# Reordering an S4 convolution's forward and backward pass on one Trainium2 core: K's chain and y first, lag sums and slabs beside dW2, every stage in a written order

## The chip, the cores and the metric

The kernel runs on one core of a Trainium2 chip. A core has engines with an instruction stream each: PE (matrix products; a weight load, PEld, comes before each matmul), DVE (elementwise and reductions), ACT (elementwise with a function), POOL (general) and SP, which in this kernel issues the DMA transfers. Each engine works its stream in order, and semaphores make one wait for another. SBUF is the memory on the core with 128 partitions, PSUM the small memory that PE writes to, DRAM the memory outside.

The metric is the device time of one execution in microseconds (us). The kernel before takes 954.58 us (median of 3 runs, 954.05 to 956.04).

## The reference

The forward pass normalizes its input, runs an S4 convolution and a two-layer network on it and multiplies the two; the kernel computes the output and the gradients of all eleven inputs.

```python
def _A_ref(u, A_re, A_im, B_re, B_im, C_re, C_im, log_dt, Dskip):
    dt = jnp.exp(log_dt)[:, None]
    logdA = dt * (A_re + 1j * A_im); dB = dt * (B_re + 1j * B_im)
    P = jnp.exp(logdA[:, :, None] * l[None, None, :])
    K = jnp.einsum("dn,dnl,dn->dl", Cc, P, dB).real
    ...
    Yf = Uf * Kf[None, :, :, :]
    y = irfft2(Yf)[..., :L]
    return y + u * Dskip

x = A_u                                # 2048 x 512
xn = _layernorm(x, axis=-1)
s = _A_ref(xn, ...)
g = _silu(_silu(xn @ w1) @ w2)         # w1: 512 x 1792, w2: 1792 x 512
return x + s * g
...
out, vjp = jax.vjp(_f, A_u, A_A_re, ..., B_w1, B_w2)
return (out, *vjp(grad_out))
```

## The kernel before, in words

Positions (2048) lie as 16 tiles t of 128 rows, channels d are 512, states n are 128. The long convolution is done with matmuls against cosine and sine tables: `TFd` for the way forward (four parts kt of 1 MB), `TId` for the way back. Both are built in the first stage and kept in DRAM.

*Stage 1* (`stage_1`, 0 to 204 us): layer norm, the network forward (L540, L515; the pre-activation h goes to DRAM as `hTd`, the transposed activation as `akd`), the tables, and powers of the state matrix, `XYd` in DRAM: 28 rows of 512 channels, real and imaginary. DS = grad_out * g is kept in SBUF.

*Stage 2* (`stage_2`): transforms of xn (`fwd_classes`, L647) and of DS (`fwd_eo`, L672) for each kt, evicted by ACT (L648, L674); DVE makes XU and XD (`rad4` L79 to L86, `add_eo` L681 to L686), stores them as `UXd` and `DXd`, and multiplies them (`cplx_mul` L94 to L98) into BK.

*Stage 3* (`stage_3`): the inverse transform of BK is the gradient of K, dK (`inv_mm` L697, eviction L828). `gs` sums it over groups of lags with selector matmuls (L818); the sums go through DRAM (`dKgd`) into `Gt`. Beside it, chunks of the table of powers are built.

A *chunk* is a quarter of the channels (32 channels by 4 positions in the layout). `ld_xy` loads its 28 rows, `chunk_tables` spreads them with nine ACT copies (L883 to L895) over X (41 columns), Y and C (16 each), and fills the rest with complex products on DVE (L902 to L904, L920). `chunk_K` multiplies C and X on PE (256 matmuls of 41 columns a chunk, L939, evicted at L941, put in order at L945) into the convolution kernel K, which goes through DRAM (`store_K` L955, `load_K` L964 to L987) into `K_b`. The layout is X[p, c, q, h, e] with c real or imaginary, q the channel group, h the column and e a parity, so what PE reads of one q lies densely.

*Stage 4* (`stage_4`, 361 to 624 us): 16 *slabs*, four a chunk, in class `Slabs`. Slab i transposes 16 groups of X and 8 of Y on PE (`P1`, L1012 and L1020; evictions L1014, L1021), builds a block matrix from Gt (`Gb`, L1029), multiplies the two (`P2`, L1041, eviction L1043), multiplies by Y on DVE (`D3`, L1052 and L1055), and sums (`P3`, L1070); results go to DRAM (`Snd`). Between the slabs stand the remaining chunks, K's way through DRAM, DMA transposes of w1 and w2 (`wt_phases`, L1098, L1102, L1107), and, from slab 10 on, K's transform (`KTransform`): the same tiles and products as for xn, with result BY.

*Stage 7* (`stage_7`): y from BY with the skip added (L694, L697), then DO = s-side gradient and the first output.

*Phase 3* (`phase_3`): here the order isn't written out; a scheduler of the framework sets it. `gen_dw2` (dW2, L1410, with akd loaded again) is mixed with `gen_conv_g` (product of KXd and DXd, inverse transform, into DXC); then `gen_ffn_bwd` (L1478 dh, transposes L1436, L1446 dx, layer norm backward), with dh kept whole in SBUF; then `gen_dw1` (L1502, eviction L1504, store `out_dram<-o10b`) and the small parameter gradients `gen_ssm_final`.

In the other stages each engine's order is the order in which the Python text emits instructions. All DMAs are issued by SP in that order, so a transfer whose data isn't ready holds those behind it. Tiles with the same `tag` share buffers: a new one waits until the last user of the old one is done. PSUM has two double tiles (`pd`) and three single ones (`ps`).

Of the kernel before, what the change touches and what calls it, by code (L numbers as in the profile page):

```python
# [124 lines left out]
def kernel(ctx, tc, A_u, A_A_re, A_A_im, A_B_re, A_B_im, A_C_re, A_C_im, A_log_dt, A_Dskip, B_x, B_w1, B_w2, grad_out,  # L125
# [20 lines left out]
    k.XYd = dr.tile([P, NT, 2, D], BF16, name="XYd")  # L146
    k.akd = dr.tile([FT, P, T, P], BF16, name="akd")
    k.hTd = dr.tile([4, P, FT, 512], BF16, name="hTd")
    k.W1Td = dr.tile([P, FT, D], BF16, name="W1Td")
    k.W2Td = dr.tile([P, DK, F], BF16, name="W2Td")  # L150
# [4 lines left out]
    k.Snd = dr.tile([2, 2, D, N], F32, name="Snd")  # L155
    k.xn = k.const.tile([P, T, D], BF16, name="xn")
    k.left = Stack(k, "left"); k.right = Stack(k, "right")
    with tc.manual_schedule():
        stage_1(k)
        stage_2(k)  # L160
        stage_3(k)
        stage_4(k)
        stage_7(k)
    phase_3(k)
    k.right.close("do")

# [78 lines left out]

class Setup:


    def __init__(self, k, W1, W2, pr, p1):
# [33 lines left out]
        k.masks = gen_masks(k, pr)  # L283
        next(k.masks)
# [38 lines left out]
    def lam(self):  # L323
        nc, k = self.k.nc, self.k
        perm = lambda ap: ap.rearrange("p (e s j w b) -> p s e j b w", e=2, s=2, j=NJ, w=4)
        pv = lambda t: t[:].rearrange("p (j s b w e) -> p s e j b w", e=2, s=2, j=NJ, w=4)
        k.lam = self.pr.tile([P, D], F32, name="lam")
        t1 = self.p1.tile([P, D], F32, name="par_t")
        nc.vector.tensor_tensor(out=t1[:], in0=k.dtb[:], in1=k.par["A_re"], op=ALU.mult)
        for s_ in range(2):  # L330
            for e_ in range(2):
                nc.scalar.activation(out=pv(k.lam)[:, s_, e_], in_=perm(t1[:])[:, s_, e_], func=ACT.Exp)
# [56 lines left out]
def power_phases(k, pr, bs, par):  # L389


    nc = k.nc
    TT = nc.vector.tensor_tensor
    perm = lambda ap: ap.rearrange("p (e s j w b) -> p s e j b w", e=2, s=2, j=NJ, w=4)
    pv = lambda t: t[:].rearrange("p (j s b w e) -> p s e j b w", e=2, s=2, j=NJ, w=4)
    SE = [(s, e) for s in range(2) for e in range(2)]
    lam = k.lam; tau = pr.tile([P, D], F32, name="tau")
    Ctr = pr.tile([P, D], F32, name="Ctr"); Cti = pr.tile([P, D], F32, name="Cti")
# [6 lines left out]
    def setup0():  # L405
        t1 = W2_("prt", "f", 2)
        nc.vector.scalar_tensor_tensor(out=t1[:, 1], in0=k.dtb[:], scalar=1.0 / (2 * math.pi), in1=g("A_im"), op0=ALU.mult, op1=ALU.mult)
        for s, e in SE:
            nc.vector.tensor_copy(out=pv(tau)[:, s, e], in_=perm(t1[:, 1])[:, s, e])

    def setup1():
# [3 lines left out]
        for (o, ba, bb, op) in ((Ctr, 0, 1, ALU.subtract), (Cti, 1, 0, ALU.add)):  # L415
            t = W2_("prt", "s", 2)
            TT(out=t[:, 0], in0=g("C_re"), in1=dB[:, ba], op=ALU.mult)
            TT(out=t[:, 1], in0=g("C_im"), in1=dB[:, bb], op=ALU.mult)
            for s, e in SE:
                TT(out=pv(o)[:, s, e], in0=perm(t[:, 0])[:, s, e], in1=perm(t[:, 1])[:, s, e], op=op)  # L420
        one = bs.tile([P, 2, 2, D], BF16, name="one", tag="XYg", bufs=2)
        nc.gpsimd.memset(one[:, 0, 0], 1.0); nc.gpsimd.memset(one[:, 0, 1], 0.0)
        nc.gpsimd.tensor_copy(out=one[:, 1, 0], in_=Ctr[:]); nc.gpsimd.tensor_copy(out=one[:, 1, 1], in_=Cti[:])
# [27 lines left out]

    def S(i):
        for j, o in st.pop(i):
            nc.sync.dma_start(k.XYd[:, j], o)

    def C(i):
        w, s = st.pop(i)
        o = bs.tile([P, 2, 2, D], BF16, name="XYg", tag="XYg", bufs=2)
        nc_ = sum(e in CEXP for e in PAIRS[i])
        if nc_ == 0:  # L460
            for c, src in ((0, w), (1, s)):
                TT(out=o[:, :, c], in0=ex[i][:], in1=src[:], op=ALU.mult)
        else:
            for c, src in ((0, w), (1, s)):
                TT(out=src[:], in0=ex[i][:], in1=src[:], op=ALU.mult)
                nc.scalar.copy(out=o[:, :, c], in_=src[:])
        st[i] = [(XIDX[e], o[:, j]) for j, e in enumerate(PAIRS[i])]
        if nc_:
            oc = bs.tile([P, 2, 2, D], BF16, name="XYg", tag="XYg", bufs=2)
            bc = lambda t: t[:].unsqueeze(1).to_broadcast([P, nc_, D])  # L470
            for c in range(2):
                c1 = W2_("c_1", "f", 2); c2 = W2_("c_2", "r", 1)
                TT(out=c1[:, 0:nc_], in0=w[:, 0:nc_], in1=bc((Ctr, Cti)[c]), op=ALU.mult)
                TT(out=c2[:, 0:nc_], in0=s[:, 0:nc_], in1=bc((Cti, Ctr)[c]), op=ALU.mult)
                TT(out=oc[:, 0:nc_, c], in0=c1[:, 0:nc_], in1=c2[:, 0:nc_], op=(ALU.subtract, ALU.add)[c])
# [84 lines left out]

def stage_1(k):
    lo, ro = k.left, k.right
    k.DS = lo.open("ds").tile([P, T, D], BF16, name="DS")
    fp = ro.open("fp"); fs = ro.open("fs", 2)
    pr = lo.open("pr"); p1 = lo.open("p1")
    W1 = fp.tile([P, DK, F], BF16, name="W1", tag="W1")
# [29 lines left out]
    put(30, lambda: next(k.masks))  # L596
# [4 lines left out]
    last = max(at)  # L601
    for n, _ in enumerate(gf, 6):
        for fn, a in at.pop(n, ()):
            fn(*a)
        if n == 28:
            TF0 = fp.tile([P, DK, F], BF16, name="TF0", tag="W1")
            k.TF0 = TF0[:].rearrange("p k f -> p (k f)")[:, 0:T * 2 * P].rearrange("p (t c q) -> p t c q", t=T, c=2)
            k.nc.sync.dma_start(k.TF0, k.TFd[0])
        if n == last:
            lo.close("bs", "tab", "pr")  # L610
            stage_2_open(k)
    assert not at


def ld_tf(k, pool, kt):
    TFs = pool.tile([P, T, 2, P], BF16, name="TFs", tag="TFs")
    k.nc.sync.dma_start(TFs[:], k.TFd[kt])
    return TFs


def ld_ti(k, pool, t0):
    ti = pool.tile([P, TS, 8, P], BF16, name="TIs", tag="TIs")
    k.nc.sync.dma_start(ti[:], k.TId[:, t0:t0 + TS])
    return ti
# [14 lines left out]
def fwd_classes(k, pool, src, TFs):  # L639

    nc = k.nc
    A = pool.tile([P, 2, 4, W], BF16, name="dA", tag="dA")
    for t1 in range(4):
        ps = k.pd.tile([P, 2, W], F32, name="ps_f", tag="pd")
        for c in range(2):
            for j in range(4):
                nc.tensor.matmul(out=ps[:, c, :], lhsT=TFs[:, t1 + 4 * j, c, :], rhs=src[:, t1 + 4 * j, :], start=(j == 0), stop=(j == 3))  # L647
        nc.scalar.copy(out=A[:, :, t1, :], in_=ps[:])  # L648
    return A


def fwd_eo(k, pool, src, TFs, TN, odd=True):

    nc = k.nc
    A = pool.tile([P, 2, 2, 2, W], BF16, name="dEO", tag="dA")
# [10 lines left out]
    for (eo, i), rows in plan.items():  # L666
        ps = k.pd.tile([P, 2, W], F32, name="ps_f", tag="pd")
        for c, terms in enumerate(rows):
            n = 0
            for t1, tab in terms:  # L670
                for j in range(4):
                    nc.tensor.matmul(out=ps[:, c, :], lhsT=tab(j), rhs=src[:, t1 + 4 * j, :], start=(n == 0), stop=(n == 4 * len(terms) - 1))  # L672
                    n += 1
        nc.scalar.copy(out=A[:, eo, :, i, :], in_=ps[:])  # L674
    return A
# [13 lines left out]
def inv_mm(k, ps, B, TIs, t0, kts, add=None, last=True):  # L689

    nc = k.nc
    for j in range(TS):
        if add is not None:
            nc.tensor.matmul(out=ps[:, j, :], lhsT=k.scI[:], rhs=add[:, j, :], start=True, stop=False)  # L694
        for kt in kts:
            for c in range(2):
                nc.tensor.matmul(out=ps[:, j, :], lhsT=TIs[:, j, 2 * kt + c, :], rhs=B[:, kt, c, (t0 + j) % 4, :],  # L697
                                 start=(add is None and kt == 0 and c == 0), stop=(last and kt == kts[-1] and c == 1))


def stage_2_open(k):
    k.fw = k.left.open("fw")
    k.fw2 = k.left.open("fw2", 2)


def stage_2(k):

    nc = k.nc
    fw, fw2, ro = k.fw, k.fw2, k.right
    w = lambda nm, shp: fw.tile(shp, BF16, name=nm, tag=nm)  # L710
    psd = k.ps.tile([P, DK, P], F32, name="ps_dsk", tag="pz", bufs=1)
    st = {}

    def front(kt):
        TFs = k.TF0 if kt == 0 else TF.pop(kt)
        st["U"] = fwd_classes(k, fw2, k.xn, TFs)
        TN = neg_tf(k, fw, TFs, kt >= 2)
        if kt < 3:
            TF[kt + 1] = ld_tf(k, fw2, kt + 1)
        return TFs, TN  # L720

    TF = {}
    fr = front(0)
    for kt in range(4):
        TFs, TN = fr
        XU, XD = w("XU", [P, 2, 4, W]), w("XD", [P, 2, 4, W])
        E, O = w("r4_e", [P, 2, 2, W]), w("r4_o", [P, 2, 2, W])
        rad4(nc, XU[:, :, 0:2], XU[:, :, 2:4], st["U"], E, O, False)
        A = fwd_eo(k, fw2, k.DS, TFs, TN, kt >= 2)
        if kt == 0:  # L730
            ro.close("fs", "fp")
            k.sa = ro.open("sa"); k.xyr = ro.open("xyr"); bk = ro.open("bk"); k.tip = ro.open("tip", 3)
            B = k.BK = bk.tile([P, 4, 2, 4, W], BF16, name="BK")
            wl, ws = wt_phases(k, fw)
        for t in range(T):
            nc.tensor.matmul(out=psd[:, kt], lhsT=k.DS[:, t, kt * P:(kt + 1) * P], rhs=k.xn[:, t, kt * P:(kt + 1) * P], start=(t == 0), stop=(t == T - 1))
        if kt < 3:
            fr = front(kt + 1)
        if kt == 0:
            k.XYc = {0: ld_xy(k, k.xyr, 0)}  # L740
        nc.sync.dma_start(k.UXd[kt], XU[:])
        add_eo(nc, XD, A, None if kt >= 2 else w("r4_o", [P, 2, 2, W]))
        if kt == 2:
            k.TI = {t0: ld_ti(k, k.tip, t0) for t0 in (0, 2, 4)}
        for i in range(2 * kt, min(2 * kt + 2, 7)):
            wl(i)
            if i:
                ws(i - 1)
        PX = cplx_mul(nc, fw, XU, XD, conj_a=True)
        nc.sync.dma_start(k.DXd[kt], XD[:])  # L750
# [809 lines left out]
```

## Time and profile before

| | us |
|---|---|
| median of 3 runs | 954.58 |
| the profiled execution | 952.84 |
| its span, first to last instruction | 951.1 |
| PE, DVE, ACT, POOL busy | 687.8, 658.3, 485.8, 42.0 |
| DMA | 153.91 MB, mean 162 GB/s |

"Busy" is the union of the times in which an engine executes something. A line such as `L1014 ACT COPY XT<-pt_xt 82x1024 ... x54 | 50.8, 1021 | 0.7 <-PE pt_xt` names the source line, engine, operation, tiles and shape, the count, the busy us in total and the mean ns of one, then the idle time just before such instructions and what ended it. "issue" is a wait for nothing that the profile shows. The clock of PE that was granted in the span is 0.88 of full speed on average.

### The profile page before, as it was taken

Reading aid. Unit: us, or ns where it says so; the run is one execution under the profiler, and the core shown is the slowest. Engines: PE = TensorE matmul, PEld = TensorE weight load, DVE = VectorE, ACT = ScalarE, POOL = GpSimd, SP = SyncE. Lnnn points to the kernel's source line nnn. Section 1 sums busy time; section 2 is a strip of 40 time slices with the busy share of each in tenths; the row PEclk is TensorE's granted clock in tenths of the full one; section 3 lists DMA queues with packets and bytes.
Section 4 is the critical chain, followed back from the end, with each engine's and each line's share of the span. In section 5 each row is a group of like instructions: output and inputs, shape, how many; then the busy total and the mean of one; then the engine's idle time right before and its main releaser. Section 6 shows DMA issues by size and latency. Waiting matters only on the chain.

```text
span 951.1 us, 13819 instructions
## 1 busy us (share of the span) xinstructions
PE 687.8 (72%) x5440; PEld 359.5 (38%) x5498; DVE 658.3 (69%) x1020; ACT 485.8 (51%) x606; POOL 42.0 (4%) x48
## 2 busy tenths in 40 slices
PE   5777676899986583425476656267668999999994
PEld 2434343444432243424363332023223445555442
DVE  7897567667979997639893187955398136777760
ACT  4578696855462446749494342213101257776341
POOL 1262211000000000000000000000000000000000
PEclk9889797999997885857698788679989999999997
DMA  8547654897584916070164423579987543332520
GB/s 246 204 149 263 234 188 159 299 333 185 175 260 138 192 27 40 12 124 12 31 173 92 132 94 110 204 290 319 361 305 235 170 125 103 95 106 57 142 62 30
DMA packets 135263, 153.91 MB, mean 162 GB/s; under 512 B 64026, under 2 KB 101021, under 8 KB 130845
## 3 DMA queue, kind: packets, MB, share of 16 engines
q1 hardware_dynamic: 135197, 153.01, 53.6%
q8 instruction: 43, 0.70, 0.3%
q14 instruction: 23, 0.19, 0.1%
HBM read 85.33 MB, written 63.98 MB: 157 GB/s over the span
## 4 chain that ended last, share of the span: by engine, by line
PE 33%; DVE 29%; ACT 16%; DMA 12%; issue 5%; SPq 2%; another core or an unknown queue 1%; POOL 0%; DVEq 0%; ACTq 0%; POOLq 0%
PE ps_f L672 8%; PE ps_v L697 5%; PE ps_da L1478 4%; PE ps_dx L1446 3%; PE ps_f L647 3%; ACT XT L1014 2%; DVE m L902 2%; DVE m L903 2%; DMA TFs<-TFd 2%; DMA out_dram<-o10b 2%; DMA TIs<-TId 1%; PE ps_h L540 1%; DVE cm_t L94 1%; DMA hTd<-hs 1%
## 5 line engine op out<-in xcount | busy, mean ns | idle before, releaser
L674 ACT CAST dEO<-ps_f 128x1024 bf16<-128x1024 f32 x32 | 32.1, 1013 | 74.1 <-PE ps_f L672 44.8
L672 PE MATMUL ps_f<-K_b,TFs 128*128 128x512 bf16 x156 | 42.6, 426 | 36.3 <-DMA TFs<-TFd 18.5
L1410 PE MATMUL ps_w<-DO_all,A_ft 128*128 128x512 bf16 x219 | 53.6, 401 | 17.4 <-DMA A_ft<-akd 16.8
L697 PEld LDWEIGHTS <-TIs 128*128 128x128 bf16 x384 | 39.2, 102 | 59.8 <-issue 20.2
L540 PE MATMUL ps_h<-XNT,W 128*128 128x512 bf16 x216 | 60.0, 421 | 2.1 <-ACT hs L543 1.2
L672 PEld LDWEIGHTS <-TFs 128*128 128x128 bf16 x296 | 30.6, 104 | 80.8 <-issue 32.6
L1012 PE MATMUL pt_xt<-ident_bfloat,X 128*82 128x128 bf16 x512 | 38.4, 232 | 30.6 <-ACT XT L1014 28.5
L1502 PE MATMUL ps_w<-dh_all,xn 128*128 128x448 bf16 x256 | 51.3, 364 | 9.8 <-ACT o10b L1504 9.8
L515 PE MATMUL ps_o<-W,aT 128*128 128x512 bf16 x215 | 52.5, 384 | 1.5 <-ACT o L519 0.9
L1478 PE MATMUL ps_da<-DOT,W2T 128*128 128x512 bf16 x216 | 52.3, 379 | 0.8 <-DVE DOT L71 0.3
L1446 PE MATMUL ps_dx<-W1T,dhT 128*128 128x512 bf16 x218 | 52.4, 379 | 0.4
L1052 DVE TENSOR_TENSOR T<-Vb,YT 128x2048 bf16<-128x2048 bf16 x16 | 19.5, 1221 | 47.7 <-PE ps_S L1070 33.0
L1014 ACT COPY XT<-pt_xt 82x1024 bf16<-82x1024 bf16 x54 | 50.8, 1021 | 0.7 <-PE pt_xt L1012 0.6
L1012 PEld LDWEIGHTS <-X 128*82 128x82 bf16 x512 | 34.0, 127 | 39.5 <-issue 39.4
L1479 DVE TENSOR_TENSOR dhT<-ps_da,sd 128x1024 bf16<-128x1024 f32 x28 | 34.2, 1221 | 18.6 <-PE ps_da L1478 15.0
L1410 PEld LDWEIGHTS <-A_ft 128*128 128x128 bf16 x224 | 22.6, 103 | 47.7 <-DMA A_ft<-akd 19.2
L121 ACT ACTIVATE sd<-hsb 128x1024 bf16<-128x1024 bf16 x28 | 29.4, 1057 | 19.1 <-DVE dhT L1479 18.1
L1502 PEld LDWEIGHTS <-xn 128*128 128x128 bf16 x256 | 25.7, 100 | 35.3 <-issue 13.2
L697 PE MATMUL ps_v<-BK,TIs 128*128 128x512 bf16 x125 | 31.9, 408 | 9.7 <-DVE BK L85 8.1
L941 ACT CAST Kt<-ps_k 128x328 bf16<-128x328 f32 x16 | 12.9, 939 | 49.8 <-PE ps_k L939 36.7
L1412 ACT CAST o11b<-ps_w 128x512 bf16<-128x512 f32 x14 | 8.2, 585 | 56.3 <-PE ps_w L1410 53.8
L672 PE MATMUL ps_f<-DS,TFs 128*128 128x512 bf16 x134 | 32.3, 393 | 3.2 <-ACT dEO L674 3.2
(316 smaller groups left out, 1585.0 us busy)
## 6 DMA issues: line engine op xcount, KB each, us to landing
TIs<-TId SPq DMA_DIRECT2D x24, 512.0 KB
hTd<-hs SPq DMA_DIRECT2D x28, 256.0 KB
akd<-ak SPq DMA_DIRECT2D x28, 256.0 KB
TFs<-TFd SPq DMA_DIRECT2D x7, 1024.0 KB
XYc<-XYd SPq DMA_DIRECT2D x4, 1792.0 KB
A_ft<-akd SPq DMA_DIRECT2D x14, 512.0 KB
hsb<-hTd SPq DMA_DIRECT2D x28, 256.0 KB
XYd<-XYg SPq DMA_DIRECT2D x25, 256.0 KB
```

Of the source, the lines that this page charges most:

```text
L515: nc.tensor.matmul(out=pso[:], lhsT=aT[:, ft, tt * P:(tt + 1) * P], rhs=W2[:, ft, :], start=(ft == 0), stop=(ft == FT - 1))
L540: nc.tensor.matmul(out=ps[:, j], lhsT=W1[:, dk, ft * P:(ft + 1) * P], rhs=XNT[:, dk], start=(dk == 0), stop=(dk == DK - 1))
L672: nc.tensor.matmul(out=ps[:, c, :], lhsT=tab(j), rhs=src[:, t1 + 4 * j, :], start=(n == 0), stop=(n == 4 * len(terms) - 1))
L674: nc.scalar.copy(out=A[:, eo, :, i, :], in_=ps[:])
L697: nc.tensor.matmul(out=ps[:, j, :], lhsT=TIs[:, j, 2 * kt + c, :], rhs=B[:, kt, c, (t0 + j) % 4, :], start=(add is None and kt == 0 and c ...
L1012: nc.tensor.transpose(out=pt[0:NR, j, :], in_=X[:, c, q0 + 8 * h + j].rearrange("p h e -> p (h e)"), identity=k.ident[:])
L1014: (nc.vector.tensor_copy if n < dv else nc.scalar.copy)(out=XT[0:NR, c, 8 * h:8 * h + 8], in_=pt[0:NR])
L1410: nc.tensor.matmul(out=ps[:], lhsT=A_ft[:, t, :], rhs=k.DO[:, t, :], start=(t == 0), stop=(t == T - 1))
L1446: nc.tensor.matmul(out=psx[:], lhsT=dhT[:, ft, tt * P:(tt + 1) * P], rhs=W1T[:, ft, :], start=(ft == 0), stop=(ft == FT - 1))
L1478: nc.tensor.matmul(out=ps[:, j], lhsT=W2T[:, dk, ft * P:(ft + 1) * P], rhs=DOT[:, dk], start=(dk == 0), stop=(dk == DK - 1))
L1479: TT(out=dhT[:, f0:f0 + 2, :], in0=ps[:], in1=sd[:], op=ALU.mult)
L1502: nc.tensor.matmul(out=ps[:], lhsT=k.xn[:, t, dk * P:(dk + 1) * P], rhs=dh_all[:, t, f0:f0 + FC], start=(t == 0), stop=(t == T - 1))
```

## The change

The diff replaces most of the text from the tables on. Its parts:

1. The sequence of stages is new, and all of it is written out. Tables, K and all transposes of X and Y come first (`stage_2`), then K's transform (`stage_3`), y mixed with the transforms of DS (`stage_4`), the inverse for dK with lag sums, then dW2 mixed with the convolution's gradient and the slabs (`stage_5`), then the network's backward pass and dW1 (`stage_6`).
2. XYd and the chunk tables have another layout, X[p, h, e, c, q]: DMAs write it directly, ACT's copies go, and what PE reads of one q has 128 elements (256 bytes) between neighbours.
3. XT and YT are made early and stored in DRAM (`XTd`, `YTd`); the slabs load them. YT takes 32 transposes of 32 columns a slab in place of 8 of 128.
4. dh goes to DRAM (`dhd`) and comes back in four column blocks for dW1. The copies of w1 and w2 in DRAM go; DMA transposes write W1T and W2T where they are used. The last quarter of dx is mixed into dW1.
5. ACT issues part of the DMAs (half of K's, all of dW2's loads).
6. Smaller: permutations of the parameters in eight pieces in place of four; masks and selectors built later; layer norm backward takes its row sum on DVE with the addition and no longer on ACT.

```diff
     with tc.manual_schedule():
         stage_1(k)
-        stage_2(k)
-        stage_3(k)
+        stage_3(k, *stage_2(k))
         stage_4(k)
-        stage_7(k)
-    phase_3(k)
+        stage_5(k)
+        stage_6(k)
...
+def ld_tab(k, b):
+    slot, cys = k.slot[b % 2]
+    X = t["X"] = slot.tile([P, NH, 2, 2, 64], BF16, name="X", tag="X")
...
+    for o, i, n in ((X[:, 0:9], 0, 9), (X[:, 16:21:4], 9, 2), (X[:, 24:31:2], 11, 4), (X[:, 32:41:8], 15, 2), (Y[:, 1:4], 17, 3), (Y[:, 0:16:4], 20, 4),
+                    (CY[:, 0:16:4], 24, 4)):
+        dma(o, k.XYd[:, i:i + n, b])
...
 def chunk_tables(k, t):
+    for o, a, b, n in ((slice(9, 16), 8, slice(1, 8), 7), (slice(17, 20), 16, slice(2, 7, 2), 3), (slice(21, 24), 20, slice(2, 7, 2), 3),
+                       (slice(25, 32, 2), 4, slice(24, 31, 2), 4), (slice(33, 34), 32, slice(8, 9), 1),
+                       (slice(34, 36), 32, slice(16, 21, 4), 2), (slice(36, 40), 32, slice(24, 31, 2), 4)):
+        TT(out=m1, in0=all_(X, al).to_broadcast([P, n, 256]), in1=all_(X, b), op=ALU.mult)
+        for c in range(2):
+            TT(out=ecq(m2)[:, :, :, c], in0=part(X, al, 1 - c).to_broadcast([P, n, 2, 64]), in1=part(X, b, c), op=ALU.mult)
+        TT(out=part(X, o, 0), in0=ecq(m1)[:, :, :, 0], in1=ecq(m1)[:, :, :, 1], op=ALU.subtract)
+        TT(out=part(X, o, 1), in0=ecq(m2)[:, :, :, 0], in1=ecq(m2)[:, :, :, 1], op=ALU.add)
...
 def chunk_K(k, b, t, pool, tag):
-                            nc.tensor.matmul(out=psk[z:z + 32, gi, :], lhsT=lt.rearrange("p l e -> p (l e)"), rhs=X[:, c, q_, :, e],
+                            nc.tensor.matmul(out=psk[z:z + 32, gi, :], lhsT=CY[:, :, :, c, q_].rearrange("p l e -> p (l e)"), rhs=X[:, :, e, c, q_],
...
+            yield
...
+def gen_xt(k, xs, i, dv):
...
+                nc.tensor.transpose(out=pt[0:NR, j, :], in_=X[:, :, :, c, q0 + 8 * h + j].rearrange("p h e -> p (h e)"), identity=k.ident[:])
+            n += 1
+            (nc.vector.tensor_copy if n > 4 - dv else nc.scalar.copy)(out=XT[0:NR, c, 8 * h:8 * h + 8], in_=pt[0:NR])
+            if n == 4:
+                nc.sync.dma_start(k.XTd[i], XT[0:NR])
+            yield
...
+def stage_2(k):
+    ld_tab(k, 1)
...
+    for b in range(2):
+        for _ in front(b):
+            if k.nt0 < 6:
+                next(k.gt[0]); k.nt0 += 1
+    for b in range(NB):
+        Kg = chunk_K(k, b, k.tabs[b], k.ps, "ps")
+        Tn = k.gt[b + 1] if b < 3 else None
+        sl = [x for i in range(4 * b, 4 * b + 4) for x in (gen_xt(k, k.xs, i, 0),) * 4] + [gen_yt(k, k.xs, i) for i in range(4 * b, 4 * b + 4)]
+        if b == 3:
+            for _ in Kg:
+                pass
+            break
+        for j, g in enumerate(sl):
+            if j == 2:
+                next(k.gt[b], None)
+            next(g)
+            if j % 2 == 0:
+                next(Kg, None)
+            if b == 0 and j in (1, 3):
+                radix(j // 2)
+            if j % 3 == 2 and j > 2:
+                next(Tn)
+        next(Tn)
+        if b < 2:
+            ld_tab(k, b + 2)
+    fr = front(2)
+    store_K(k)
...
+    load_K(k, K_b)
+    next(k.gt[3])
...
+    for _ in fr:
+        pass
+    radix(2)
+    for _ in front(3):
+        pass
+    radix(3)
...
+def stage_3(k, K_b, sl):
...
+    for n, _ in enumerate(gen_kt(k, kq, K_b, UX)):
+        for g in (next(sl, None) for _ in range(3)):
+            if g is not None:
+                next(g)
...
+def stage_4(k):
+    gd = gen_d(k, k.bk, k.kq)
...
+    for t0 in range(0, T, TS):
+        if t0 % 4 == 0:
+            for _ in range(2):
+                next(gd)
...
+        inv_mm(k, ps, [k.BY[:, i] for i in range(4)], TI, t0, (0, 1, 2, 3), add=y.ins[t0]["XD"])
+        if t0 and t0 + 2 < T:
+            y.pre(t0 + 2)
...
+        o = y.out(t0, S_s)
+        if t0 + 4 < T:
+            y.load(t0 + 4)
+        nc.sync.dma_start(*o)
+        if t0 % 4 == 0:
+            next(gd); next(gd)
+        elif t0 + 2 < T:
+            for _ in range(3):
+                next(gd)
...
+def stage_5(k):
...
+        inv_mm(k, ps, k.BK, k.TI.pop(t0), t0, (0, 1, 2, 3))
...
+        if t0 % 4 == 0:
+            pr.mul(kt)
+        else:
+            pr.rad(kt, BG[:, kt])
...
+        if t0 >= 2:
+            gs(t0 - 2)
...
+    for ft in range(FT):
+        t0 = 2 * (ft - 3)
+        if 0 <= t0 < T:
+            if t0 + 2 < T:
+                skip(t0 + 2)
+            conv(t0)
+            some(1)
+        for _ in w2.run(ft):
+            some(2 if t0 >= 0 else 0)
+        some(2 if t0 >= 0 else 0)
+        if ft % 2 == 1:
+            j = ft // 2
+            nc.sync.dma_start_transpose(k.W2T[:, :, 256 * j:256 * j + 256], k.ins["w2"][256 * j:256 * j + 256])
...
+    def steps(self):
+        self.Gb(0)
+        for i in range(16):
+            self.P2(i, 0)
+            if i + 1 < 16:
+                self.Gb(i + 1)
+            yield
+            self.P2(i, 1)
+            if i + 2 < 16:
+                self.load(i + 2)
+            yield
+            self.D3(i)
+            if i:
+                self.P3(i - 1)
+            if i > 1 and i % 4 == 1:
+                self.store(i // 4 - 1)
+            yield
...
+def stage_6(k):
...
+    for n in range(28):
+        B.dh(n)
+        if n < 7:
+            nc.sync.dma_start_transpose(W1T[:, 2 * n:2 * n + 2], k.ins["w1"][:, 256 * n:256 * n + 256])
+        next(prev, None)
+        if n == 25:
+            ld_ch(0)
+        if n % 7 == 6:
+            if n < 27:
+                B.dot(n // 7 + 1)
+            for _ in prev:
+                pass
...
+            prev = B.dx(n // 7, B.dhT)
...
+    for i in range(4):
+        for dk in range(DK):
+            next(prev, None)
+            for t in range(T):
+                nc.tensor.matmul(out=ps[:], lhsT=k.xn[:, t, dk * P:(dk + 1) * P], rhs=ch[i][:, t, :], start=(t == 0), stop=(t == T - 1))
+            nc.scalar.copy(out=ob[:], in_=ps[:])
+            next(prev, None)
...
+        if i + 2 < 4:
+            ld_ch(i + 2)
```

In the excerpt, `gen_kt` and `gen_d` yield after each forward tile, after the additions, after the product and after the radix step of a part kt; `w2.run` yields in the middle of its 16 matmuls; `some(n)` runs n steps of the slabs; `front` yields after each of its four tiles; `B.dh` makes two blocks of dh and sends the ones before to DRAM.

## The prediction

> **What bounds the kernel now.** I first read the busy times of the whole span: no engine is above 72%, so no single engine is the limit and the waits between stages have to be found.
>
> ```profile
> span 951.1 us, 13819 instructions
> PE 687.8 (72%) x5440; PEld 359.5 (38%) x5498; DVE 658.3 (69%) x1020; ACT 485.8 (51%) x606; POOL 42.0 (4%) x48
> ```
>
> Then I cut the span at its stages. The columns are length, busy time and instruction count of each engine, clock, DMA share and GB/s. The cuts are: feed-forward pass, transforms of xn and DS, gradient of K with lag sums, tables and slabs (361 to 500), K's transform with slabs (500 to 624), y, dW2 with the convolution's gradient, backward, dW1.
>
> ```profile
> core 0: us, PE busy (x) PEld busy (x) DVE busy (x) ACT busy (x) POOL busy (x), PEclk, DMA share, GB/s
> 0.00:204.00 204.00, 146.41 (x901) 78.30 (x919) 153.80 (x288) 144.89 (x186) 41.13 (x44) 0.90 0.67 225
> 204.00:303.00 99.00, 86.33 (x424) 40.27 (x432) 82.40 (x106) 46.39 (x49) 0.91 (x4) 0.93 0.69 201
> 303.00:361.00 58.00, 38.73 (x424) 18.41 (x428) 54.95 (x95) 28.87 (x34) 0.00 (x0) 0.85 0.55 116
> 361.00:500.00 139.00, 67.31 (x1729) 54.37 (x1729) 103.83 (x162) 96.24 (x113) 0.00 (x0) 0.73 0.41 68
> 500.00:624.00 124.00, 64.35 (x485) 31.34 (x488) 80.45 (x95) 40.47 (x42) 0.00 (x0) 0.79 0.41 139
> 624.00:673.00 49.00, 36.49 (x141) 14.76 (x142) 25.73 (x39) 13.75 (x14) 0.00 (x0) 0.90 0.84 296
> 673.00:770.00 97.00, 82.63 (x355) 36.14 (x364) 51.40 (x56) 15.25 (x21) 0.00 (x0) 0.95 0.73 256
> 770.00:888.00 118.00, 115.42 (x736) 60.98 (x749) 79.68 (x135) 80.98 (x106) 0.00 (x0) 1.00 0.31 88
> 888.00:951.00 63.00, 50.09 (x251) 24.95 (x249) 26.06 (x48) 18.96 (x46) 0.00 (x0) 0.92 0.30 79
> ```
>
> The hole is 361 to 624: 263 us in which the busiest engine, DVE, works 184. The backward stage (115 of 118 on PE) holds nothing to win. The waits in 361 to 470 (total us, times, longest) and the longest pieces of the chain say why:
>
> ```profile
> PEld L939 <- issue: 39.6, 11, 12.8
> ACT Kt L941 <- PE ps_k L939: 27.2, 4, 14.2
> PE ps_k L939 <- DVE CY L904: 19.5, 2, 12.6
> ```
> ```profile
> 372.16 12.99 another core or an unknown queue
> ...
> 489.02 10.72 DMA TFs<-TFd
> ...
> 610.49 5.78 DMA TIs<-TId
> 616.29 8.21 DMA TIs<-TId
> ```
>
> K's small matmuls (L939) stand in PE's queue until the table products on DVE are done, or starve with nothing to wait for; K's way through DRAM and the load of its table, then the first loads of y, end the other gaps.
>
> **The change, stage by stage.** I sum the busiest engine in each new stage with the durations of this trace, add the waits that the new order leaves, and so walk through the span.
>
> *Feed-forward pass, now 204 us.* The parameter permutations get twice the instructions on half the elements (8 more on DVE near L420's 0.38 us, 4 more on ACT near 0.42): at most 5 us, beside 50 us of idle DVE; the mask building (about 5 us of small DVE operations at 1.6 us) leaves the start. I take 0, bounds -2 to +5. Three table steps of chunk 0 (7 us of DVE) now lie in its last ticks.
>
> *Tables, K, and the transposes, new: 204 to 358.* Table work on DVE per chunk: rows fit 0.154 us + elements/1.92 GHz (1024: 0.68, 2048: 1.22). Products for X: 18432 elements in 35 instructions, 15.0; C and Y, 5.4 each: 25.8 us, against 26.8 before. On ACT the nine copies that spread a chunk (L883 to L895, about 9.5 us) are gone, since seven DMAs write the layout; but all 16 XT evictions (L1014, 1.02) come to ACT, with 4 of YT (1.03), 4 of K (0.94) and 1.85 of K's reordering: 26 us. Four DMAs of 672 KB and four of 256 KB per chunk store XT and YT for later, and 1.8 MB are loaded, about 10 us at the 200 to 230 GB/s of before's load of the same bytes (405 to 416 us). PE first runs xn's transforms (64 matmuls at 0.216, 14 us), waits for chunk 0 until 227 (load landed about 207, then 20 us of products), then: chunk 0 with the products of chunk 1 and two radix steps (5.3 each) 37 us of DVE; two rounds of 26 + 6, as the load of chunk 2 and 3 starts only when a slot is free and DVE has 6 us of nothing: chunk_K(3) at 327, done 336. K's round trip took 32 us before (467.6 to 500); its 22 loads now go out on SP and ACT together and the table is loaded already: I take 22, to 358, bounds 15 to 32. ACT issues half of them, so the evictions of the last 14 us of xn's transforms queue behind; they are not late for anything until K_b is there.
>
> *K's transform, 358 to 451.* Four forward tiles (48 matmuls, 10.4 us) with 12 transposing steps on ACT: 22. Then per part on DVE: additions 4.0 (L681 to L686), product 7.2 (2.29 + 4 x 1.22, L94 to L98), radix 5.3: 16.5 x 4 = 66, plus 2.5 where PE and ACT still have 8 steps, 2.7 for y's first two preparations. 93.
>
> *y with DS, 451 to 550.* DVE per pair of y tiles: 16.5 for one part of DS (15 for the last two) and 2 x 3.4 for y (five operations at 0.68): four pairs 90. PE needs 79 (368 matmuls). 5 at the start, where y(0) has only PE, 4 for loads: about 25 MB in 99 us, 250 GB/s, where y moved 296 before and waited. The sum is 99, bounds 92 to 110. The old y (49) and DS's half of 204 to 303 go away.
>
> *Gradient of K, dW2, convolution, slabs, 550 to 720.* Inverse and lag sums need 180 matmuls (39 us), beside DVE's products for the convolution (50, and 5 for the selectors) and 12 MB of loads: PE 45. Three dW2 tiles (10) cover the way of the sums through DRAM; this was masked before, and I leave 6 uncovered. Then per dW2 tile: convolution 18 x 0.216 = 3.9, dW2 3.45, 1.67 slabs at 2.34 (ps_V 18.7 and ps_S 18.7 over 16) = 3.9; 8 tiles 90, three more 20. Sum 170. DVE needs 69 there (Gbd 1.36, T 2.6 per slab), ACT 52, so both hide. What hides them is PE; without it, 58 us of slab work would show, as in 361 to 560 now.
>
> *Backward and dW1, 720 to 898.* Start: the slabs' last store puts 8 DMAs (0.63 us each on SP) ahead of the first loads of h: 6. PE: L1478 and L1446 48.4 each, transposes 17 and 5, dW1 256 x 0.189 = 48.4: 168. The stall of 15.8 us at 919.7, where o10b waits for its store, goes, as dx of the last quarter is mixed into dW1; dh's way through DRAM (7.3 MB twice) is covered by 12 us of PE per quarter. End 4. Sum 178, 181 before.
>
> **Sum:** 204 + 154 + 93 + 99 + 170 + 178 = 898 us of span. The profiled execution took 952.84 for 951.1, so 1.7 lie around the span: 900. Two costs have no row. PE now reads X, Y and C with 256 bytes between elements, for 512 XT transposes, 512 small YT ones (128 before) and 1024 of K. Nearest rows:
>
> ```profile
> L1014 ACT COPY XT<-pt_xt 82x1024 bf16<-82x1024 bf16 x54 | 50.8, 1021 | 0.7 <-PE pt_xt L1012 0.6
> L332 ACT ACTIVATE lam<-par_t 128x128 f32<-128x128 f32 x4 | 1.4, 418 | 2.0 <-DVE par_t L329 2.0
> L941 ACT CAST Kt<-ps_k 128x328 bf16<-128x328 f32 x16 | 12.9, 939 | 49.8 <-PE ps_k L939 36.7 <-remote 13.0
> L1504 ACT CAST o10b<-ps_w 128x448 bf16<-128x448 f32 x16 | 8.3, 524 | 31.2 <-DMA out_dram<-o10b 21.6 <-PE ps_w L1502 9.6
> ```
>
> L332 reads SBUF with 16 bytes between elements and pays 7% over the dense 390 ns of L1348; L941, which reads PSUM and writes with gaps, pays 2.4 ns an element where dense rows (448: 524, 1024: 1013) pay 0.85, a factor of 2.85. Dense, a chunk costs PE 20 us (transposes 0.112 each at half clock, eight in 0.91 us at 362.5; YT a quarter each; K 256 in 2.2). SBUF reads are nearer to L332, so little is lost beside 26 to 37 us: bounds 0 and 84. The other cost is starved PE: "issue" ends 5% of the chain, 50 us. The largest such wait from 361 to 470 is L939's, which is now cut into pieces of 64 between transposes; bounds -5 to +25. For both I add 4. That gives 904 against 952.84; the median of 954.58 lies 1.7 higher, so **906**, 5% faster.
>
> [...]
>
> **The rivals.** *Strided reads bind PE (slower).* At L941's factor a chunk takes 57 us on PE (41 + 10 + 6): 20 + 25 + 25 over the rounds above and 14 for chunk 3, +84: 990. It decides from about 2.4 times dense (47 us a chunk), where the gain of 49 is gone. [...] Against: L332, and ACT paces XT at 128 ns a transpose, more than dense PE needs. *Starved PE and collisions:* the starved 50 us remain although DVE hides less, and more traffic (some 37 MB more than 154) delays loads: +36, 942. For: the 12.99 us piece has no releaser while small gathers run; against: share 0.41 in that stage. *Denser mixing:* stages overlap at their seams, the 22 of K, 6 + 6, 12 of loads and the idle 9 before chunk 0 vanish: 906 - 45 = 861. For: dW2 already runs at 85% of PE; against: each seam is a true dependence. *The order doesn't hide the slabs:* one SP queue carries some 90 more DMAs, and a load behind a waiting store stops PE's order; if half of the 58 shows, 935.
>
> **Chances.** Forecast 0.50 (own range 878 to 930), denser 0.14, the two middle rivals together 0.20, strided 0.16. The measurement cannot tell 0.2% (1.9 us) from no change. Slower: 0.16 and 0.03 from the upper end of the middle rivals, 0.19; same 0.02; faster 0.79. The range leaves out strided and the lowest of denser: 858 to 958.
>
> **What would show it.** Right: XT evictions at 1.02 us back to back in 227 to 330; DVE above 85% in K's transform and in y; PE above 90% in dW2 with slabs; no wait above 10 us in dW1. Wrong: LDWEIGHTS from X above 200 ns and ACT waiting for pt_xt; PE ended by "issue" for over 50 us before K's transform; K_b later than 30 us after the last K eviction; slabs waiting for loads of XT; dh's loads ending waits of dW1.

## The result and the profile after

The changed kernel takes 1243.46 us (median of 4 runs, 1240.52 to 1248.7) against 954.32 for the kernel before on the same chip (4 runs): a ratio of 1.3043, interval 1.2981 to 1.3105. It is 289 us slower, where 858 to 958 was the range of the prediction. The busy times, from the first lines of the page:

```profile
span 1238.7 us, 14811 instructions
PE 792.1 (64%) x5811; PEld 431.6 (35%) x5882; DVE 636.2 (51%) x1011; ACT 471.5 (38%) x566; POOL 65.8 (5%) x57
```

DVE and ACT have slightly less work than before. PE is busy 104 us longer: XT's transposes alone went from 38.4 us (L1012 before) to 76.5 (L791 now), and the granted clock of the span fell from 0.88 to 0.81. But no engine is busy more than 64% of the span, so most of the time went into waits. The windows by stage show where (same columns as in the prediction; the cuts are the load and building of tables, K and transposes, K's transform, y, the gradient of K with dW2 and slabs, backward with dW1):

```profile
204.00:473.00 269.00, 129.37 (x1965) 107.55 (x1967) 117.34 (x240) 100.54 (x108) 20.49 (x11) 0.70 0.34 110
473.00:602.00 129.00, 84.72 (x487) 47.87 (x496) 62.23 (x92) 48.48 (x48) 0.00 (x0) 0.81 0.47 170
602.00:685.00 83.00, 74.87 (x312) 32.21 (x318) 73.29 (x91) 29.70 (x32) 0.26 (x1) 0.90 0.73 256
685.00:1041.00 356.00, 183.92 (x1187) 77.60 (x1207) 129.75 (x167) 61.78 (x72) 4.15 (x4) 0.75 0.61 133
1041.00:1238.00 197.00, 169.17 (x961) 86.87 (x975) 105.97 (x183) 86.49 (x118) 0.00 (x0) 0.94 0.61 169
```

The first, second and fourth rows hold the loss; in the first, no engine works half of the time and the DMA share is 0.34. The third row has no transfer of XT or YT, and it alone runs as foreseen. The chain of waits from 204 to 480 names the transfers (start, length, what; a piece ends when the store has landed):

```profile
253.04 21.38 DMA XTd<-XT
280.47 21.17 DMA YTd<-YT
320.10 18.68 DMA XTd<-XT
344.56 21.47 DMA YTd<-YT
384.62 18.62 DMA XTd<-XT
409.31 21.31 DMA YTd<-YT
```

In the list of groups the same is seen from the engines that wait, ACT for the stores and PE for the loads:

```profile
L1444 PE MATMUL ps_V<-XTl,Gbd 82*32 82x256 bf16 x512 | 28.6, 379 | 119.2 <-DMA XTl<-XTd 116.2
L791 PEld LDWEIGHTS <-X 128*82 128x82 bf16 x512 | 75.1, 233 | 59.5 <-issue 57.2
L793 ACT COPY XT<-pt_xt 82x1024 bf16<-82x1024 bf16 x64 | 66.5, 1083 | 72.1 <-DMA XTd<-XT 67.5
L809 ACT COPY YT<-pt_yt 128x1024 bf16<-128x1024 bf16 x16 | 18.3, 1204 | 86.5 <-DMA YTd<-YT 86.5
L680 DVE TENSOR_TENSOR m<-X 128x768 bf16<-128x768 bf16 (+4 forms) x28 | 18.3, 653 | 93.8 <-DMA X<-XYd 93.7
```

XT has 82 rows, YT 128. A store of 656 KB (units of 1024) that takes 18.7 us comes to 36 GB/s. YT's 256 KB take as long; they stand behind XT's in SP's queue, and the table products on DVE wait for loads of X in the same queue. How many of the 16 DMA engines work during such a store is told by one window, 255 to 273 us, in which almost nothing but stores of XT is under way:

```profile
255.00:273.00 18.00, 4.62 (x32) 4.58 (x32) 8.78 (x8) 3.75 (x4) 0.00 (x0) 0.59 0.13 53
```

The DMA share, second from the end, is 0.13, what two engines of sixteen come to (0.125), at 53 GB/s. At that rate 656 KB take 12.7 us. The first piece above is longer because the store before it, issued at 243.77 us, ends only at 259; from 252 to 259 the share is 0.12 already, at 50 GB/s. The theory for the experiments is therefore: *two engines carry XT, and all that stands behind it waits.* That the 82 rows are the cause was the author's guess; this row doesn't show it, and e1 and e11 put it to the test. Its rivals are the strided reads of the prediction (PEld of L791 takes 233 ns where before took 127), and a cost of the written order itself.

### The profile page after: what moved, and what is told of

It reads as the page before. It is cut to its first block, busy times and chain, and to the rows that moved or that the text cites. A ratio compares the mean times of both kernels' runs of the same rounds, so it can differ in the third digit from the quotient of the medians.

```text
span 1238.7 us, 14811 instructions
## 1 busy us (share of the span) xinstructions
PE 792.1 (64%) x5811; PEld 431.6 (35%) x5882; DVE 636.2 (51%) x1011; ACT 471.5 (38%) x566; POOL 65.8 (5%) x57
## 2 busy tenths in 40 slices
DMA packets 147811, 199.58 MB, mean 161 GB/s; under 512 B 36698, under 2 KB 106973, under 8 KB 139997
## 4 chain that ended last, share of the span: by engine, by line
DMA 38%; PE 28%; DVE 16%; ACT 8%; SPq 6%; issue 4%; ACTq 0%; POOL 0%; DVEq 0%; POOLq 0%
DMA XTl<-XTd 10%; DMA YTd<-YT 7%; DMA XTd<-XT 7%; PE ps_v L954 4%; PE ps_da L1550 3%; PE ps_f L928 3%; PE ps_dx L1589 3%; SPq L1406 3%; PE pt_xt L791 3%; DMA out_dram<-o10b 2%; DMA TIs<-TId 2%; DMA YTl<-YTd 2%; PE ps_k L718 2%; DVE XYg L469 1%; ACT XT L793 1%
## 5 line engine op out<-in xcount | busy, mean ns | idle before, releaser
L791 PE MATMUL pt_xt<-ident_bfloat,X 128*82 128x128 bf16 x512 | 76.5, 316 | 57.0 <-ACT XT L793 56.6
L1455 DVE TENSOR_TENSOR T<-Vb,YTl 128x2048 bf16<-128x2048 bf16 x16 | 19.6, 1225 | 181.6 <-ACT Vb L1446 159.4
L1444 PE MATMUL ps_V<-XTl,Gbd 82*32 82x256 bf16 x512 | 28.6, 379 | 119.2 <-DMA XTl<-XTd 116.2
L791 PEld LDWEIGHTS <-X 128*82 128x82 bf16 x512 | 75.1, 233 | 59.5 <-issue 57.2
L793 ACT COPY XT<-pt_xt 82x1024 bf16<-82x1024 bf16 x64 | 66.5, 1083 | 72.1 <-DMA XTd<-XT 67.5
L1446 ACT CAST Vb<-ps_V 128x1024 bf16<-128x1024 f32 x32 | 31.7, 1013 | 145.9 <-PE ps_V L1444 115.0
L1668 PE MATMUL ps_w<-dhc,xn 128*128 128x448 bf16 x256 | 55.3, 379 | 16.2 <-ACT o10b L1670 16.2
L718 PE MATMUL ps_k<-X,CY 128*32 128x41 bf16 x1024 | 26.9, 278 | 59.6 <-ACT YT L809 59.6
L1299 PE MATMUL ps_w<-DO_all,AW 128*128 128x512 bf16 x213 | 62.9, 451 | 2.3 <-issue 2.3
L928 PEld LDWEIGHTS <-TFs 128*128 128x128 bf16 x336 | 34.9, 106 | 76.5 <-issue 27.2
L822 PE MATMUL ps_f<-xn,TFs 128*128 128x512 bf16 x125 | 33.1, 427 | 35.0 <-ACT XU L823 18.8
L718 PEld LDWEIGHTS <-CY 128*32 128x32 bf16 x1024 | 24.8, 156 | 60.6 <-issue 59.8
```

The lines of the kernel that those rows point to most:

```text
L718: nc.tensor.matmul(out=psk[z:z + 32, gi, :], lhsT=CY[:, :, :, c, q_].rearrange("p l e -> p (l e)"), rhs=X[:, :, e, c, q_], start=(c == 0), ...
L791: nc.tensor.transpose(out=pt[0:NR, j, :], in_=X[:, :, :, c, q0 + 8 * h + j].rearrange("p h e -> p (h e)"), identity=k.ident[:])
L793: (nc.vector.tensor_copy if n > 4 - dv else nc.scalar.copy)(out=XT[0:NR, c, 8 * h:8 * h + 8], in_=pt[0:NR])
L1299: nc.tensor.matmul(out=ps[:], lhsT=A[:, t, :], rhs=k.DO[:, t, :], start=(t == 0), stop=(t == T - 1))
L1444: nc.tensor.matmul(out=ps[32 * w:32 * w + 32, b4], lhsT=G[0:NR, q, g2].rearrange("p b c -> p (b c)"), rhs=XT[0:NR, :, q, :], start=True, s ...
L1668: nc.tensor.matmul(out=ps[:], lhsT=k.xn[:, t, dk * P:(dk + 1) * P], rhs=ch[i][:, t, :], start=(t == 0), stop=(t == T - 1))
```

## The experiments

**e1, XT in two pieces.** Store and load of XT are cut at row 80; nothing else changes.

```diff
-                nc.sync.dma_start(k.XTd[i], XT[0:NR])
+                nc.sync.dma_start(k.XTd[i, 0:80], XT[0:80])
+                nc.sync.dma_start(k.XTd[i, 80:NR], XT[80:NR])
...
-        nc.sync.dma_start(XT[0:NR], k.XTd[i])
+        nc.sync.dma_start(XT[0:80], k.XTd[i, 0:80])
+        nc.sync.dma_start(XT[80:NR], k.XTd[i, 80:NR])
```

> Same bytes as the changed kernel, but each XT store and XT load goes out as two DMAs, rows 0 to 79 and rows 80 and 81, in place of one of 82 rows. Theory A (a transfer of 82 rows is spread over few DMA engines, so that 656 KB take 15 to 20 us each, and everything in SP's queue stands behind it): the 82-row transfers fall to 3 to 5 us; the waits of ACT for XTd and YTd stores (154 us) and of PE for XTl (116 us) nearly vanish; 930 to 980 us. Theory B (the new traffic of 37 MB and the longer SP queue are too much): the bytes are the same and SP has 32 DMAs more, so 1235 to 1260 us. Theory C (PE's strided reads bind the stage): 1235 to 1250 us.

Measured: 964.47 us, ratio 1.0141 (1.0103 to 1.0178): 279 of the 289 us are gone. The experiments ran in three groups (e1 to e4, e5 to e8, e9 to e11) on three chips, where the kernel before took 951.21, 956.33 and 951.96 us, so differences between groups are good to some 5 us; the ratios take that out. Windows of e1, cut at the same events:

```profile
204.00:379.00 175.00, 130.19 (x1972) 107.69 (x1973) 125.28 (x242) 103.43 (x112) 19.01 (x11) 0.83 0.59 176
379.00:480.00 101.00, 78.81 (x490) 46.24 (x500) 63.61 (x91) 49.25 (x48) 0.00 (x0) 0.93 0.72 220
480.00:562.00 82.00, 72.00 (x312) 31.38 (x317) 73.06 (x91) 29.71 (x32) 0.26 (x1) 0.94 0.73 256
562.00:765.00 203.00, 157.01 (x1186) 68.87 (x1206) 129.37 (x167) 61.59 (x72) 4.16 (x4) 0.89 0.80 233
765.00:961.00 196.00, 167.59 (x961) 86.05 (x975) 105.88 (x183) 86.52 (x118) 0.00 (x0) 0.95 0.61 170
```

94, 28 and 153 us less in the first, second and fourth rows, with the same bytes, the same work and twice the number of DMAs for XT; the other two rows stand. YT's stores weren't touched, and ACT's waits for them in the first row fall from 60.5 to 8.2 us: they were slow only for what stood ahead of them. Of PE's 104 us of additional busy time 39 are gone (753.3 us at a clock of 0.90); 49 more go in e4 below (704.0).

**e2 and e3, one side alone.** e2 cuts only the stores, e3 only the loads.

> Only the 16 XT stores are split into 80 and 2 rows, the loads stay at 82 rows. Theory A: the stage with tables and K falls from 269 us to 155 to 175 and K's transform by some 25, the slabs stay at 245: 1090 to 1130 us. Theories B and C: 1235 to 1255 us.

> Only the 16 XT loads are split into 80 and 2 rows, the stores stay at 82 rows. Theory A: the 50 us before the first slab and 120 us of the slabs vanish, the first stages stay as they are: 1060 to 1110 us. Theories B and C: 1235 to 1255 us.

Measured: e2 1115.06 us, ratio 1.1718 (1.1662 to 1.1773); e3 1090.88, ratio 1.1463 (1.1407 to 1.152). The stores are worth 128 us, the loads 153; together 281, where both at once gave 279. They lie in different stages (K's transform starts at 376.7 us in e2 and at 475.3 in e3) and add up.

**e11, two pieces of 41 rows.** This tells the number of rows in a piece from the size and the number of the DMAs: as many pieces as e1 and the same bytes, but 41 rows in each.

```diff
-                nc.sync.dma_start(k.XTd[i], XT[0:NR])
+                nc.sync.dma_start(k.XTd[i, 0:41], XT[0:41])
+                nc.sync.dma_start(k.XTd[i, 41:NR], XT[41:NR])
...
-        nc.sync.dma_start(XT[0:NR], k.XTd[i])
+        nc.sync.dma_start(XT[0:41], k.XTd[i, 0:41])
+        nc.sync.dma_start(XT[41:NR], k.XTd[i, 41:NR])
```

> The changed kernel with each XT transfer cut into two DMAs of 41 rows instead of 80 and 2. If the size of one DMA or the number of its packets made the transfer slow, the halves would be as good as the cut at 80: 960 to 990 us. If the rows are spread over as many engines as divide them, 41 rows go to one engine each, and two DMAs reach two engines at best, as 82 rows did: 1230 us or more, up to 1800 if both land on one engine.

Measured: 1633.33 us (2 runs), ratio 1.7139 (1.7065 to 1.7213), 390 us slower still. A window of e11 during such a store:

```profile
260.00:270.00 10.00, 0.00 (x0) 0.00 (x0) 4.14 (x4) 0.00 (x0) 0.00 (x0) 0.50 0.06 27
```

A share of 0.06 is what one engine of sixteen comes to (0.0625), at 27 GB/s, half of the 53 above. Both halves of the first store are issued by 244.5 us, and it ends only at 272; in the changed kernel, at a share of 0.13, it ended at 259. So the two halves together moved at the rate of one engine; which one no run shows. The first XT store on the chain lasts 46.09 us instead of 21.38. So in these cuts the number of rows decides, not the size or the number of the DMAs: e1 (ratio 1.0141) has as many DMAs as e11 (1.7139), and its piece of 80 rows, 640 KB, is hardly smaller than the 656 KB of 82.

**e4, PE reading densely.** e1, and PE's reads of X, Y and CY (K's matmuls and all transposes) take neighbouring elements. These are other elements of the tables, so the outputs aren't the reference's: the run gives the price of the reads and is no kernel to use. One of the three places:

```diff
-                nc.tensor.transpose(out=pt[0:NR, j, :], in_=X[:, :, :, c, q0 + 8 * h + j].rearrange("p h e -> p (h e)"), identity=k.ident[:])
+                nc.tensor.transpose(out=pt[0:NR, j, :], in_=X[:].rearrange("p h e c q -> p (h e c q)")[:, 82 * (q0 + 8 * h + j) + 5248 * c:82 * (q0 + 8 * h + j) + 5248 * c + 82], identity=k.ident[:])
```

> As e1_split, and PE reads X, Y and C densely (neighbouring elements, the same counts) for the XT and YT transposes and for K's matmuls; so K, XT and YT are filled from other elements and the outputs aren't the reference's. Theory A alone: within 10 us of e1_split. Theory C (strided reads cost PE 2 times or more and PE then paces the tables' stage): 20 to 60 us faster than e1_split; the weight loads from X go from about 235 ns to about 127 ns.

Measured: 941.25 us, ratio 0.9865 (0.9806 to 0.9925); 23 us below e1 (by the ratios 26). The weight loads tell why; the group of e4 that answers to L791's above:

```profile
L791 PEld LDWEIGHTS <-X 128*82 128x82 bf16 x512 | 40.5, 140 | 18.9 <-issue 15.5
```

140 ns instead of 233, 1.66 times, and CY's 32 columns (L718) fall from 156 to 103 ns. The strided reads are a real cost, but a twelfth of XT's.

**e5 and e6, two columns of single elements.** In e1 the chain still shows two pieces that are out of proportion to their bytes:

```profile
416.93 16.19 DMA YTd<-YT
```
```profile
929.98 15.84 DMA out_dram<-o10b
```

Before each, SP has issued a store of 512 values of 2 bytes each, which go to DRAM as single elements: out_9 in K's transform, out_8 in the last stage. The kernel before has the same two stores, followed by the pieces of 12.99 us (of unknown queue, quoted in the prediction) and of 15.78 us. e5 turns both columns to 4 rows of 256 bytes on PE; e6 leaves them and has ACT's queue issue them.

```diff
+def store_col(k, pool, o, col):
+    nc = k.nc
+    pt = k.ps.tile([P, 8, P], BF16, name="pt_col", tag="ps")
+    nc.tensor.transpose(out=pt[0:DK, 0, :], in_=col, identity=k.ident[:])
+    row = pool.tile([DK, P], BF16, name=f"row{o}")
+    nc.scalar.copy(out=row[:], in_=pt[0:DK, 0, :])
+    nc.sync.dma_start(k.outs[o].rearrange("(k p) -> k p", p=P), row[:])
...
-            nc.sync.dma_start(k.outs[9].rearrange("(k p) -> p k", p=P), dskb[:])
+            store_col(k, kq, 9, dskb[:])
...
-    nc.sync.dma_start(k.outs[8].rearrange("(k p) -> p k", p=P), ob[:])
+    store_col(k, fp, 8, ob[:])
```

> The changed kernel with each XT transfer cut at row 80 (964 us in its own run), and the two outputs of 512 two-byte values (out_8 and out_9) turned to 4 rows of 256 bytes on PE before they are stored, instead of 512 single elements. Theory: the single elements hold up what follows them, 16.19 us on the chain after out_9's store in K's transform and 15.78 us before o10b's store at the end; without them 25 to 32 us are gone, 930 to 942 us. Rival: these waits are those of the DMAs that are named in them (a read of fresh data, a last store), and the time stays within 4 us of 964.

> The changed kernel with each XT transfer cut at row 80, and the stores of out_8 and out_9, still as single elements, issued by ACT's queue instead of SP's. If the single elements hold up only the queue that they stand in, this gains what the version with rows gains, 25 to 32 us. If they hold up the DMA engines themselves, whatever the queue, it gains little, 0 to 8 us. If they have nothing to do with the waits: within 4 us of 964.

Measured on one chip: e5 952.03 us, ratio 0.9945 (0.9918 to 0.9973); e6 970.16, ratio 1.0132 (1.0087 to 1.0177), where e1 had 1.0141. Rows gain about 0.0196 of 951, 19 us, less than the 25 to 32 expected; another queue gains nothing. With ACT's queue both pieces are still on e6's chain:

```profile
417.10 14.83 DMA YTd<-YT
936.92 17.09 DMA out_dram<-o10b
```

What happens in such a piece is told by a window of e1, in the middle of the second:

```profile
940.00:943.00 3.00, 0.01 (x1) 0.00 (x0) 0.00 (x0) 0.00 (x0) 0.00 (x0) 1.00 0.00 0
```

A store of o10b is waited for, until 945.82, and the DMA engines move nothing. So the single elements hold up the transfers of other queues too, not only those of their own; by what, no run shows. A load of 512 single elements doesn't do it: from 866 to 876 us in e1, right after that of `ldt` (L1185, issued at 861.75), the DMA engines move 309 GB/s, and in the changed kernel, which issues it at 1138.94, 305 GB/s from 1143.2 to 1153.2. Both 16 us pieces are gone from e5's chain, but at the end o10b still waits 20.6 us for its stores (33.0 in e1), in pieces of 5.73 and 7.83, so part of the gain is not kept.

**e9, the same rows in the kernel before.**

> The kernel before, with its own two stores of 512 single elements (out_9 in K's transform, out_8 in the last stage) turned to rows of 256 bytes. It has the same two waits as the changed kernel: the chain shows 15.78 us before o10b's store right after out_8's, and 12.99 us of an unknown queue after out_9's. If single elements hold up the DMA engines in any kernel: 12 to 29 us less than before, 924 to 942 us. If the waits come from how the changed kernel is ordered: within 4 us of before.

Measured: 935.9 us against 951.96, ratio 0.9816 (0.9783 to 0.9849), 16 us less. The piece of 12.99 us is gone from its chain, and the last piece of work is now whole, dW1's 256 matmuls without the stop:

```profile
880.61 48.44 PE ps_w L1511 x256
```

Of the kernels whose computation is unchanged, this is the fastest, and it needs nothing of the change.

**e7 and e8, the order at the seam.** After e1 the seam before the first slab is the next large gap. e7 moves the loads of Gt right behind dKgd's stores, ahead of the slabs' loads; e8 has that, e5's rows, and YT's stores on ACT's queue.

```diff
-    S.load(0); S.load(1)
...
-    ld(0); ld(2); ld(4)
...
+    ld(0)
+    S.load(0)
+    ld(2)
+    S.load(1)
+    ld(4)
```

> The changed kernel with each XT transfer cut at row 80, and at the seam before the gradient of K the loads of Gt issued right behind dKgd's stores, ahead of the slabs' loads. Theory: 31 us of the seam (617 to 648) are loads that stand behind other loads in SP's queue, and 8 to 15 us of it go: 949 to 957 us. Rival: the first slab needs its own load as late as it needed Gt, and the order only changes which of them is last: within 4 us of 964.

> All of it together: XT's transfers cut at row 80, out_8 and out_9 stored as rows, the loads of Gt first at the seam, and YT's stores on ACT's queue instead of SP's. If the three gains are real and add up, 33 to 50 us below 964, 914 to 931 us, which is faster than the kernel before by 2 to 4 per cent. Rival: the stretches are bound by bytes and the order of the queues only moves the wait: 945 to 964 us, no better than the kernel before.

Measured: e7 970.54 us, ratio 1.0132 (1.0083 to 1.0181), nothing against e1. Gt now lands sooner, and the chain goes on with YTl (9.62 us) and AW's store (9.29) instead: the rival was right, the order only changes which transfer is last. e8 962.0, ratio 1.0053 (1.0025 to 1.0081), is 10 us worse than e5. The loss is there before K's transform: the last matmul of K starts at 350.6 us in e8 and at 340.2 in e5, and the waits for YT's store on the chain are 6.34, 6.32 and 9.73 us against 3.66, 3.86 and 3.70. Why a store issued by ACT took longer there was not tried further.

**e10, all three costs away.** e1, e5's rows and e4's dense reads.

> The changed kernel with all three costs taken away that were found so far: XT's transfers cut at row 80, PE reading X, Y and CY densely (K, XT and YT are then filled from other elements), and out_8 and out_9 stored as rows. If the three are separate and add up: 279 + 23 + 19 us below the changed kernel's 1243, about 917 to 928 us, 3 per cent faster than the kernel before. Rival: strided reads and single elements cost the same time twice (both lie in K's transform), and the sum stays at 930 to 942 us.

Measured: 925.74 us, ratio 0.9713 (0.9683 to 0.9744). Against e5 that is 22 us for the dense reads, as between e1 and e4: the three costs are separate. Like e4, e10 reads other elements, so it is a price and no kernel to use: the change without its three costs would be worth some 26 us against the kernel before, and 10 us against the kernel before with rows (0.9816).

## Why the prediction was wrong

The stages of the sum beside the profiled executions (us; the cuts are the first matmul of K's transform, the end of PE's wait for the last BY, the end of its wait for the last BK, the first matmul of dh):

| stage | forecast | after | e1 | e10 |
|---|---|---|---|---|
| forward pass, tables, K, transposes | 358 | 473.5 | 379.2 | 357.7 |
| K's transform | 93 | 133.6 | 105.4 | 87.5 |
| y with DS | 99 | 92.3 | 91.5 | 91.6 |
| gradient of K, dW2, convolution, slabs | 170 | 342.0 | 189.2 | 190.0 |
| backward and dW1 | 178 | 197.3 | 196.3 | 194.9 |
| span | 898 | 1238.7 | 961.6 | 921.7 |

*The step that failed* is the sentence "Four DMAs of 672 KB and four of 256 KB per chunk store XT and YT for later", and with it "What hides them is PE" for the slabs' loads. The transfers were counted, but got no time of their own. Where the sum prices a transfer, it takes 200 to 250 GB/s whatever its shape; this step it left at the price nothing. A store of 82 rows ran at a DMA share of 0.13 and 53 GB/s, takes about 19 us on the chain, and in a queue worked in order it delays YT's stores, the loads of the next chunk's X and, later, the loads of TIs, XE and W2T. Measured: 128 us for the stores, 153 for the loads. The sign "slabs waiting for loads of XT" was there (116.2 us of PE's waits). The bytes were short as well (46 MB more than before, where "some 37" was forecast), but e1 moves the same 199.58 MB. The rival "the order doesn't hide the slabs" had the right place, a load that stops PE's order behind one SP queue, but its price, half of 58 us, came from the slabs' work and not from a transfer. No row of the trace of before had a DMA of 82 rows, and the prediction didn't say that this cost lacks a row: it bounded two such costs, and left out the third and largest.

*The claim of back-to-back evictions of XT from 227 to 330* was wrong in the changed kernel (ACT waited 67.5 us for XTd); in e1 that wait is 1.0 us.

*The stage to 358.* With dense reads it ends at 357.7, where the sum had 358, but that is luck: two errors cancel. In e10 K's last matmul starts at 320.5 us and its last eviction ends at 322, where the sum had K done at 336. Then 36 us pass until K's transform starts, where the sum had 22. The chain of e10 shows them:

```profile
324.38 5.44 DMA Kud<-Kout
330.94 4.64 DMA K_b<-Kud
339.68 5.11 PE ps_f L823 x16
350.75 6.86 DMA TFs<-TFd
```

K's loads are quick: their last piece on the chain ends at 338.6. But ACT, which issues half of them, waits 15 us meanwhile and evicts the last tile of xn's transforms only then. The store of its result stands in SP's queue ahead of the load of the table, which the sum had "loaded already". So the clause on those evictions, "they are not late for anything until K_b is there", failed. In the changed kernel the same pieces follow one another from 439.67 to 473.42 us.

*Strided reads.* The sum took at most 4 us for it, with 0 and 84 as bounds; measured 22 to 26. L332, the row that was taken as nearest, was an ACT row and too kind; L941's factor of 2.85 was too hard: the weight loads of the same 82 columns take 233 ns against 140, a factor of 1.66. The sign that the prediction named, LDWEIGHTS above 200 ns, was there.

*The stall of 15.8 us* was to go "as dx of the last quarter is mixed into dW1". It stayed in e1 (15.84), because it never came from the order: it follows 512 single elements. The prediction took a wait for a store as a matter of cover without asking what the DMA engines did meanwhile. The rest of the last stage is as forecast on PE (168.8 busy in e10, 168 forecast); PE's further waits there are 14.3 us for o10b and 5.8 for dhc.

*The gradient of K* took 190 where 170 was forecast, even in e10. The seam that was to leave "6 uncovered" takes 30 us; the chain of e10:

```profile
578.25 3.83 DMA dKgd<-gs_o
...
582.23 9.50 DMA AW<-akd
...
592.11 5.03 DMA XTl<-XTd
...
600.69 7.68 DMA Gt<-dKgd
```

The way of the lag sums through DRAM shares the engines with the loads of dW2 and of the first slabs, and each of these is waited for in turn. e7 shows that the order of SP's queue doesn't change this; the DMA share in that stage of e10 is 0.80, but whether fewer bytes would help was not tried.

*What held:* y at 92 (forecast 99, its lower bound 92), K's transform at 87.5 without its foreign costs (93, though DVE is busy 75% there and not above 85), and, with the three costs away, the direction: 0.9713 measured where 906 would have been 0.949.

## What to carry to other kernels

Cost a new DMA by the rate that a transfer with its number of rows reaches, before its bytes: 82 rows ran at a DMA share of 0.13 and 53 GB/s and cost 279 us here, 41 and 41 rows at 0.06 and 27 GB/s, and cut into 80 and 2 rows the same bytes were nearly hidden. A slow transfer costs more than its own time, because a queue that is worked in order passes it on to transfers that have nothing to do with it (ACT's waits for YT's stores before K's transform, 60.5 us, were 8.2 in e1), so look for the waits behind it. Where a store of a few bytes is followed by a wait of many microseconds (here 1 KB and some 16 us), look at the size of its pieces. And where one stage of a forecast comes out to the microsecond, look whether its parts did.

## What the runs showed of the hardware beyond the question

- Two DMAs of 41 rows together moved at a DMA share of 0.06 and 27 GB/s, one of 82 rows at 0.13 and 53 GB/s: cutting a transfer in the wrong place made the kernel 390 us slower.
- A store of 512 single elements of 2 bytes (1 KB in all) holds back other transfers for some 16 us, from SP's queue (16.19 and 15.84 us in e1) as from ACT's (14.83 and 17.09 in e6); as 4 rows of 256 bytes it left no such piece on the chain, and after a load of 512 single elements the DMA engines moved 309 GB/s.
- With loads of 82 rows in SP's queue even the issue of others is slow: the DMA transposes of W2T take SP 1.27 us each in e1 (median of 7) and 12.96 in the changed kernel, up to 17.4; in e3, where only the loads are cut, at most 1.9:

```profile
862.20 17.39 SPq L1406 DMA_TRANSPOSE W2T<-in_B_w_dram  x1
```
